# One-bank PSUM tiles, 512-token units and two more weights decoded early, in a fused attention, expert and gated-MLP kernel

## The chip, the cores and the metric

The kernel runs on one core of one Trainium2 chip. The metric is the device time of one execution in microseconds (us). Before the change it is 957.31 us, the median of three runs (956.15 to 957.85).

## The reference

Four batches of 576 tokens with 8 heads of 64 go through kernelized attention, then an expert layer, then a gated MLP; all in float32.

```python
def phi(x):
    proj = np.einsum('bhsd,df->bhsf', x, w_phi)                  # 64 -> 128
    proj = proj - np.max(np.abs(proj), axis=-1, keepdims=True)
    return np.concatenate([np.exp(proj), np.exp(-proj)], axis=-1)
kv = np.einsum('bhsf,bhsd->bhfd', k_p, v); z = np.sum(k_p, axis=2)
attn = num / den                                                # 2304 x 512 in all
e_idx = argmax(x @ w_gate)                                      # 8 experts, 512 -> 1024 -> 512
out[mask] = gate_w * eom * (np.maximum(x[mask] @ w1[e], 0) @ w2[e])
xn = x / rms * rms_g
out = (silu(xn @ w_gate) * (xn @ w_val)) @ w_out                # 512 -> 1536 -> 512
```

## The kernel before

There are two stages. **Stage 1** does attention, the gate and the expert layer for the four batches (0 to 3). Expert products start while the attention of the next batch still runs. The kernel guesses one expert per batch and computes all its tokens with it; a branch behind the stage (`general`, L899) would do the rest and is not entered by these inputs. **Stage 2** is the gated MLP. It goes over the 2304 tokens in units of `UT` = 384, six in all, in the order 0, 5, 1, 2, 3, 4 (L1031).

Nothing here is ordered by the compiler: each stage puts tasks with an engine, a modelled duration, a priority and the buffers they read and write into a `Graph` (L42). `emit` (L121) takes the task that can start first, and the instructions of each engine then stand in that order. A task also needs a free slot of each buffer tag it writes. The engines run their queues in order; semaphores follow from the tiles an instruction touches.

A float32 product is made of three float32r products (high by high, high by low, low by high). So weights and activations are kept as pairs, made by a cast on ACT and a subtraction on DVE. The MLP weights come as 64-bit floats: `decode` (L770) loads 128x1024 words into a `raw` buffer (two of them) and turns them into a pair, by one ACT instruction (L777), three of DVE (L779, L782, L785), a cast on ACT (L788) and a subtraction on DVE (L789). One step f of the MLP needs two decodes for gate and value (`decode_gv`, L792) and one for the output weights (`decode_o`, L799). Six of the twelve steps (`NPRE`) have their gate and value weights decoded in stage 1; all other decodes run during the first unit of stage 2.

`unit` (L846) does, for each of 12 steps, gate and value products (2 x 12 matmuls of 128x384, L860), silu on ACT (L866), the product with the value on DVE (L868), a cast (L870) and a subtraction (L871), then for each 128 tokens three output matmuls of 128x512 (L878). `prep` (L802) normalizes the tokens of the next unit into `xn` pairs, with one matmul for the mean square (L832).

PSUM has eight banks of 512 float32 per partition. `psum` (L299) makes four tiles of one bank (`ps0` to `ps3`) and two tiles of two banks each (`pq0`, `pq1`). The two-bank tiles take the projections of the attention (tag `pp`), which DVE reads whole (L414, L416). After nine projections `pq1` is taken out of `pp` and its two halves go to `ph`, the tag of the expert products (`mm1` L675, `mm2` L685), which then has three banks: `ps3` and the two halves of `pq1`. In stage 2 the gate and value products use `ps3` and three halves of `pq1` and `pq0`:

```python
self.ps = one + [t[:, i] for t in self.two[::-1] for i in range(2)]     # L303
self.g.retire("pp", 9, self.two[1], "ph", [self.two[1][:, i] for i in range(2)])   # L310
g.slot("po", kk.ps[0:3]); g.slot("pgv", kk.ps[3:7]); g.slot("pms", kk.ps[7:8])     # L1020 to L1022
```

In an expert product of 128x288 (12 matmuls, L682, or 24, L691) ACT and DVE read the bank afterwards: ACT L729 and DVE L731 make the pair `h`, DVE L743 makes `y`. Each step of the expert weights is itself a cast on ACT of 128x1024 (L712) and a subtraction on DVE (L713).

All transfers are issued from SP's queue. At the start these are the two halves of `w_phi` (L296), then keys, values and the left-over 64 tokens of each head (L367, L373, L382, L388).

Of the kernel before, what the change touches and what calls it, by code (L numbers as in the profile page):

```python
# [22 lines left out]
DM = H * D  # L23
P = 128
# [17 lines left out]
class Graph:  # L42
# [22 lines left out]
    def free_slot(self, b):  # L65
        self.slots[b.tag].append((b.end, b.slot[1], b.slot[2]))
        rule = self.leaving.get(b.tag)
        if rule:
            rule[0] -= 1
            for f in [f for f in self.slots[b.tag] if f[2] is rule[1] and rule[0] <= 0]:  # L70
                self.slots[b.tag].remove(f)
                n = 100 + len(self.slots[rule[2]])
                self.slots[rule[2]].extend((f[0], n + i, a) for i, a in enumerate(rule[3]))
                del self.leaving[b.tag]
# [153 lines left out]
class K:  # L228
# [62 lines left out]
    def attn_consts(self, c):  # L291
# [3 lines left out]
        for i in range(2):  # L295
            self.g.t("SP", 0.6, lambda i=i: nc.sync.dma_start(self.wraw[i * D:(i + 1) * D], self.w_phi),  # L296
                     w=[self.cBw], prio=0.5, nbytes=1 << 15)

    def psum(self, ctx):  # L299
        ps = self.pool(ctx, "ps", space=PSUM)  # L300
        self.two = [ps.tile([P, 2, 512], F32, name=f"pq{i}") for i in range(2)]
        one = [ps.tile([P, 512], F32, name=f"ps{i}") for i in range(4)]
        self.ps = one + [t[:, i] for t in self.two[::-1] for i in range(2)]  # L303
        self.g.slot("pa", one[0:3])
        self.g.slot("pp", self.two)
        self.g.slot("ph", one[3:4])

    def halve(self):

        self.g.retire("pp", 9, self.two[1], "ph", [self.two[1][:, i] for i in range(2)])  # L310
# [8 lines left out]
    def moe_slots(self, ctx):  # L319
        p = self.pool(ctx, "moe", side="right")  # L320
        self.moe_consts(p)
        self.mk(p, "xh", 2, [P, 2, NC, S], F32R)
# [35 lines left out]
    def attn(self, b, prio):  # L358
# [3 lines left out]
        xp = [Buf(None, 0) for _ in range(NC + 1)]  # L362

        def load(src, pr, np_):
# [6 lines left out]
            for i, m in enumerate((self.k, self.q)):  # L371
                for j in range(2):
                    g.t("SP", 0.6, lambda i=i, j=j, m=m: nc.sync.dma_start(  # L373
                        t.ap[j * 64:(j + 1) * 64, i], m[b, j::2, MAIN:S].rearrange("h t d -> t h d")),
                        w=[t], prio=np_, nbytes=LEFT * H * D * 2)
# [73 lines left out]
        el = vl = None  # L449
        for i, pr in enumerate([0, "L", 1, 2, 3]):  # L450
# [18 lines left out]
            if el is None:  # L469
                continue  # L470
            for pr, e, v, np_ in ready:
                pk, ks, pz = g.buf("pa"), g.buf("ks"), g.buf("pa")
                for j in range(2):
                    def kvm(j=j, pr=pr, e=e, v=v, pk=pk):
                        ops = [(v.ap[:, j, c], e.ap[:, at(j, c)]) for c in range(NC)]
                        ops.append((vl.ap[:, j, pr], el.ap[:, (pr % 2) * 2 + pr // 2]))
                        return [partial(nc.tensor.matmul, pk.ap[0:D + 1, j * 256:(j + 1) * 256], lhsT=v_,
                                        rhs=e_.rearrange("p f e -> p (f e)"), start=(n == 0), stop=(n == NC))
                                for n, (v_, e_) in enumerate(ops)]
                    g.t("PE", 5 * 0.431, kvm, r=[e, v, el, vl], rw=[pk], prio=np_, kind="pass", steps=5)  # L480
# [271 lines left out]
    def phase2_slots(self, ctx):  # L752
# [3 lines left out]
        self.xn = [p.tile([P, 2, UT], F32R, name=f"xn{i}") for i in range(NXN)]  # L756
        self.sq = p.tile([P, 2, UT], F32, name="sq")
        self.rm = p.tile([P, 2, UT], F32, name="rm")
        self.raw = [p.tile([P, 1024], U32, name=f"raw{i}") for i in range(2)]
        self.tt = [p.tile([P, 512], F32, name=f"tt{i}") for i in range(2)]  # L760
        self.ww = [p.tile([P, 512], F32, name=f"ww{i}") for i in range(3)]
# [3 lines left out]
    def use_phase2(self, g):  # L765
        for tag, aps in (("yu", [self.y]), ("sq", [self.sq]), ("rm", [self.rm]), ("raw", self.raw), ("tt", self.tt),
                         ("ww", self.ww)):
            g.slot(tag, aps)

    def decode(self, g, src, dst, dstap, prio):  # L770

        nc = self.nc
        raw, tt, ww = g.buf("raw"), g.buf("tt"), g.buf("ww")
# [14 lines left out]
        g.t("ACT", act(512, False), lambda: nc.scalar.copy(dstap(0), ww.ap), r=[ww], w=[dst], prio=prio)  # L788
        g.t("DVE", dve(512), lambda: nc.vector.tensor_tensor(out=dstap(1), in0=ww.ap, in1=dstap(0), op=ALU.subtract),  # L789
            r=[ww], rw=[dst], prio=prio)  # L790

    def decode_gv(self, g, f, prio):  # L792
        for i, m in enumerate((self.mg, self.mv)):
            src = (lambda ap: ap.rearrange("p (c n) -> p c n", c=NC),
                   m[:, f * 256:(f + 1) * 256].rearrange("(c p) n -> p c n", p=P))
            self.decode(g, src, self.wgv[f], lambda a, i=i, f=f: self.wgv[f].ap[:, i, a].rearrange("p c n -> p (c n)"),
                        prio)
# [4 lines left out]
    def prep(self, g, u, prio, hold=False):  # L802

        nc = self.nc
        y, sq, ms, rm = g.buf("yu"), g.buf("sq"), g.buf("pms"), g.buf("rm")
        g.t("SP", 0.5, lambda: nc.sync.dma_start(y.ap, self.ydr[:, :, u * UT:(u + 1) * UT]),
            r=self.yB, w=[y], prio=prio, nbytes=P * NC * UT * 4)
        self.prep_rest(g, y, sq, ms, rm, prio)
        xn = []
        for c in range(NC):  # L810
            x = g.buf("xn", hold)
            xn.append(x)
            g.t("DVE", dve(UT), lambda c=c: nc.vector.scalar_tensor_tensor(  # L813
                out=y.ap[:, c], in0=y.ap[:, c], scalar=self.gcol[:, c:c + 1], in1=rm.ap[:, 0],
                op0=ALU.mult, op1=ALU.mult), r=[rm], rw=[y], prio=prio)
        for c in range(NC):
            x = xn[c]
            g.t("ACT", act(UT, False), lambda x=x, c=c: nc.scalar.copy(x.ap[:, 0], y.ap[:, c]), r=[y], w=[x], prio=prio)
            g.t("DVE", dve(UT), lambda x=x, c=c: nc.vector.tensor_tensor(  # L819
# [247 lines left out]
```

## Time and profile before

| | |
|---|---|
| median of three runs | 957.31 us (956.15 to 957.85) |
| the profiled execution: its own time, its span | 959.13 us, 957.5 us |
| mean granted clock of TensorE | 0.989 of full speed |
| busy: TensorE matmul, weight load | 914.5 us (96%), 835.9 us (87%) |
| busy: VectorE, ScalarE, GpSimd | 433.9 us (45%), 337.4 us (35%), 3.2 us |
| matmul instructions | 6044 |
| first gate product of stage 2 starts | 485.70 us |

The names are those of the profile: PE is TensorE's matmul, PEld its weight load, DVE VectorE, ACT ScalarE, POOL GpSimd, SP the queue that issues transfers. Busy time of PE is modelled and overlaps a little from one matmul to the next, so how fast matmuls follow each other is read from the starts of pieces in order of time, not from the mean length of one. An idle time stands with the work that ended last before it.

### The profile page before, as it was taken

Reading aid. Unit: us, or ns where it says so; the run is one execution under the profiler, and the core shown is the slowest. Engines: PE = TensorE matmul, PEld = TensorE weight load, DVE = VectorE, ACT = ScalarE, POOL = GpSimd, SP = SyncE. Lnnn points to the kernel's source line nnn. Section 1 sums busy time; section 2 is a strip of 40 time slices with the busy share of each in tenths; the row PEclk is TensorE's granted clock in tenths of the full one; section 3 lists DMA queues with packets and bytes.
Section 4 is the critical chain, followed back from the end, with each engine's and each line's share of the span. In section 5 each row is a group of like instructions: output and inputs, shape, how many; then the busy total and the mean of one; then the engine's idle time right before and its main releaser. Section 6 shows DMA issues by size and latency. Waiting matters only on the chain. (4 is left out here: it accounts for less than half of the span.)

```text
span 957.5 us, 14539 instructions
## 1 busy us (share of the span) xinstructions
PE 914.5 (96%) x6044; PEld 835.9 (87%) x6045; DVE 433.9 (45%) x826; ACT 337.4 (35%) x588; POOL 3.2 (0%) x23
## 2 busy tenths in 40 slices
PE   7988999999999998999989799999999999999998
PEld 5677799789889997898988789999999998999997
DVE  4454565556444547884248882322323133132111
ACT  4343435534433325543145551322223123122111
POOL 1000000000000000000000000000000000000000
PEclk9997999999999999999999989999999999999999
DMA  5313513421511146673145440002001002000000
GB/s 147 105 56 109 139 47 117 143 62 45 180 56 55 49 159 200 181 231 102 48 135 156 148 139 34 1 1 67 1 1 66 1 1 67 1 1 34 1 1 34
DMA packets 84984, 74.60 MB, mean 78 GB/s; under 512 B 30256, under 2 KB 78512, under 8 KB 84400
## 3 DMA queue, kind: packets, MB, share of 16 engines
q1 hardware_dynamic: 84912, 73.60, 25.2%
q8 instruction: 50, 0.82, 0.4%
q14 instruction: 22, 0.18, 0.1%
HBM read 54.63 MB, written 18.96 MB: 77 GB/s over the span
## 5 line engine op out<-in xcount | busy, mean ns | idle before, releaser
L860 PE MATMUL pq<-xn,wgv 128*128 128x384 f32 x1296 | 240.0, 338 | 12.3 <-DVE sil L868 12.3
L860 PEld LDWEIGHTS pq<-xn,wgv 128*128 128x128 f32 x1296 | 227.1, 189 | 18.5 <-DVE sil L868 9.2
L878 PE MATMUL ps<-wo,a 128*128 128x512 f32 x648 | 160.5, 392 | 0.0
L868 DVE TENSOR_TENSOR sil<-pq,sil 128x384 f32<-128x384 f32 x71 | 39.6, 557 | 223.9 <-PE pq L860 223.9
L878 PEld LDWEIGHTS ps<-wo,a 128*128 128x128 f32 x648 | 120.7, 188 | 22.0 <-DVE a L871 0.2
L860 PE MATMUL ps<-xn,wgv 128*128 128x384 f32 x432 | 81.2, 335 | 2.5 <-PEq L914 2.5
L860 PEld LDWEIGHTS ps<-xn,wgv 128*128 128x128 f32 x432 | 75.9, 188 | 5.3 <-issue 2.7
L682 PE MATMUL pq<-xh,w 128*128 128x288 f32 x492 | 73.3, 300 | 7.4 <-DVE h L731 7.1
L691 PE MATMUL pq<-h,w 128*128 128x288 f32 x528 | 76.5, 298 | 2.8 <-DVE y L743 2.2
L870 ACT CAST a<-sil 128x384 fp32r<-128x384 f32 x72 | 36.8, 512 | 118.7 <-DVE sil L868 118.7
L682 PEld LDWEIGHTS pq<-xh,w 128*128 128x128 f32 x492 | 66.4, 188 | 10.7 <-DVE h L731 7.5
L691 PEld LDWEIGHTS pq<-h,w 128*128 128x128 f32 x528 | 71.3, 188 | 4.4 <-DVE y L743 3.1
L209 PE MATMUL ps<-kv,qp 128*128 128x65 f32 x512 | 69.2, 276 | 5.7 <-DVE x L444 4.5
L209 PEld LDWEIGHTS ps<-kv,qp 128*128 128x128 f32 x512 | 67.6, 201 | 7.8 <-DVE x L444 4.9
L414 DVE TENSOR_REDUCE m<-pq 128x8 f32<-128x1024 f32 x36 | 43.9, 1223 | 49.6 <-PE pq L410 45.9
L209 PE MATMUL ps<-e,v 128*65 128x256 f32 x256 | 63.2, 389 | 0.7 <-ACT e L465 0.7
L871 DVE TENSOR_TENSOR a<-sil,a 128x384 fp32r<-128x384 f32 x72 | 39.9, 555 | 28.8 <-ACT a L870 28.4
L209 PEld LDWEIGHTS ps<-e,v 128*65 128x65 f32 x256 | 35.0, 142 | 19.3 <-issue 1.8
L712 ACT CAST w<-wr 128x1024 fp32r<-128x1024 f32 x32 | 33.5, 1047 | 45.6 <-PE pq L691 18.5
L713 DVE TENSOR_TENSOR w<-wr,w 128x1024 fp32r<-128x1024 f32 x32 | 39.2, 1224 | 20.5 <-ACT w L712 19.8
L866 ACT ACTIVATE sil<-ps 128x384 f32<-128x384 f32 x35 | 17.2, 491 | 85.6 <-PE ps L860 85.6
L433 ACT ACTIVATE qp<-ps 128x512 f32<-128x512 f32 x64 | 34.7, 598 | 33.6 <-PE ps L209 30.1
(141 smaller groups left out, 985.7 us busy)
## 6 DMA issues: line engine op xcount, KB each, us to landing
wr<-in_moe_w SPq DMA_DIRECT2D x32, 512.0 KB, 3.7
xdr<-xh SPq DMA_DIRECT2D x4, 2304.0 KB, 9.4
raw<-in_moe_w_gate SPq DMA_DIRECT2D x12, 512.0 KB, 3.5
raw<-in_moe_w_val SPq DMA_DIRECT2D x12, 512.0 KB, 4.2
raw<-in_moe_w_out SPq DMA_DIRECT2D x12, 512.0 KB, 3.7
yu<-ydr SPq DMA_DIRECT2D x6, 768.0 KB, 4.9
qk<-in_k SPq DMA_DIRECT2D x16, 256.0 KB, 3.5
v<-in_v SPq DMA_DIRECT2D x32, 128.0 KB, 2.6
```

Of the source, the lines that this page charges most:

```text
L209: f()
L414: g.t("DVE", dve(1024), lambda: nc.vector.tensor_reduce(out=m.ap, in_=pv(), axis=AX.X, op=ALU.max, apply_absolute_value=True), r=[pp], w=[ ...
L433: g.t("ACT", act(512), lambda f=f: nc.scalar.activation(qp.ap[:, f].rearrange("p c t -> p (c t)"), pd.ap, AF.Exp, scale=1.0 - 2.0 * f), r= ...
L682: self.nc.tensor.matmul(ph[:, 0:HS], lhsT=wv[:, a, c, fs], rhs=xh[:, x, c, cs], start=(c == 0 and i == 0), stop=(c == NC - 1 and i == 2))
L691: self.nc.tensor.matmul(ph[:, 0:HS], lhsT=wv[:, a, f], rhs=hs[f][:, x, cs], start=(f == 0 and i == 0), stop=(f == 7 and i == 2))
L712: g.t("ACT", act(1024, False), lambda: nc.scalar.copy(w.ap[:, 0], wr.ap), r=[wr], w=[w], prio=pr - AHEAD)
L713: g.t("DVE", dve(1024), lambda: nc.vector.tensor_tensor(out=w.ap[:, 1], in0=wr.ap, in1=w.ap[:, 0], op=ALU.subtract), r=[wr], rw=[w], prio= ...
L860: nc.tensor.matmul(ps.ap[:, 0:UT], lhsT=w[:, i, a, c], rhs=xn[c].ap[:, x], start=(c == 0 and n == 0), stop=(c == NC - 1 and n == 2))
L868: g.t("DVE", dve(UT), lambda sil=sil, ps=pgv[1]: nc.vector.tensor_tensor(out=sil.ap, in0=ps.ap[:, 0:UT], in1=sil.ap, op=ALU.mult), r=[pgv[ ...
L870: g.t("ACT", act(UT, False), lambda sil=sil, a=a: nc.scalar.copy(a.ap[:, 0], sil.ap), r=[sil], w=[a], prio=pr)
L871: g.t("DVE", dve(UT), lambda sil=sil, a=a: nc.vector.tensor_tensor(out=a.ap[:, 1], in0=sil.ap, in1=a.ap[:, 0], op=ALU.subtract), r=[sil], ...
L878: nc.tensor.matmul(po[t].ap, lhsT=a.ap[:, x, ts], rhs=w[:, y], start=(f == 0 and n == 0), stop=(f == NF - 1 and n == 2))
```

## The change

- PSUM is made of one-bank tiles wherever a half is used by itself. When `pq1` leaves `pp`, its pool is closed and a new pool with two one-bank tiles (`ph0`, `ph1`) takes its place; before stage 2 all pools are closed and eight one-bank tiles (`pz0` to `pz7`) are made, four for output (`po`), four for gate and value (`pgv`). The mean square of `prep` has no bank of its own any more and takes one of `pgv`.
- Stage 2 has units of 512 tokens: four of them, and one of 256 (the left-over tokens of all batches), in the order 0, 4, 1, 2, 3. There are four `xn` tiles instead of five.
- The gate and value weights of steps 6 and 7 are decoded in stage 1, into a buffer `xh` that held the tokens of a batch (`keep`, `part`). Four decodes leave the first unit of stage 2.
- Scratch tiles are shared: eight tiles `row` of 128x512 for what were `tt`, `ww`, `sil`, `osb` and `rm`; the squares of `prep` are kept in a `raw` buffer.
- The key-value products of the first pair of heads are split: the part of the main tokens is issued before the left-over tokens are there.
- In batch 0 the two loads of `w_phi` and the four loads of left-over keys and queries are issued from ACT's queue instead of SP's.

```diff
-    def psum(self, ctx):
+    def psum(self):
+        self.banks, self.pair = ExitStack(), ExitStack()
+        p = self.pool(self.banks, "ps", space=PSUM)
+        one = [p.tile([P, 512], F32, name=f"ps{i}") for i in range(4)]
+        two = [p.tile([P, 2, 512], F32, name="pq0"),
+               self.pool(self.pair, "pq", space=PSUM).tile([P, 2, 512], F32, name="pq1")]
...
     def halve(self):
-        self.g.retire("pp", 9, self.two[1], "ph", [self.two[1][:, i] for i in range(2)])
+        self.pair.close()
+        p = self.pool(self.pair, "ph", space=PSUM)
+        return [p.tile([P, 512], F32, name=f"ph{i}") for i in range(2)]
+    def psum2(self, ctx):
+        self.pair.close()
+        self.banks.close()
+        p = self.pool(ctx, "pz", space=PSUM)
+        return [p.tile([P, 512], F32, name=f"pz{i}") for i in range(8)]
...
-            self.g.t("SP", 0.6, lambda i=i: nc.sync.dma_start(self.wraw[i * D:(i + 1) * D], self.w_phi),
-                     w=[self.cBw], prio=0.5, nbytes=1 << 15)
+            self.g.t("ACT", 0.6, lambda i=i: nc.scalar.dma_start(self.wraw[i * D:(i + 1) * D], self.w_phi),
+                     w=[self.cBw], prio=-2, nbytes=1 << 15)
...
+        eng, dma = ("ACT", nc.scalar.dma_start) if b == 0 else ("SP", nc.sync.dma_start)
...
             if el is None:
+                first = g.buf("pa")
+                for j in range(2):
+                    kv_part(j, *ready[0], first, range(NC))
                 continue
...
+    def part(self, f):
+        n = 4 * NC * P
+        return self.kept.ap.rearrange("p a c s -> p (a c s)")[:, (f - NPRE) * n:(f - NPRE + 1) * n].rearrange(
+            "p (i a c n) -> p i a c n", i=2, a=2, c=NC)
...
     def prep(self, g, u, prio, hold=False):
-        y, sq, ms, rm = g.buf("yu"), g.buf("sq"), g.buf("pms"), g.buf("rm")
+        y, sq, ms, rm, ri = g.buf("yu"), g.buf("raw"), g.buf("pgv"), g.buf("row"), g.buf("row")
...
-UT = 384
-NU = B * S // UT
-NXN = 5
+UT = 512
+NROW = 8
+NU = 5
 NPRE = 6
+NKEEP = 2
+def width(u):
+    return UT if u < B else B * LEFT
...
+        kk.kept = g.buf("xh", hold=True)
+        for f in range(NPRE, NPRE + NKEEP):
+            kk.decode_gv(g, f, 2000 + f, [kk.kept])
...
-    g.slot("po", kk.ps[0:3])
-    g.slot("pgv", kk.ps[3:7])
-    g.slot("pms", kk.ps[7:8])
+    g.slot("po", banks[0:4])
+    g.slot("pgv", banks[4:8])
```

The order moves on every engine, since the planner makes it anew. Three places count here.

On PE, at the first expert product of batch 2 (line L682, now L706), the names are the PSUM tiles that are written. Before:

```order
L682 MATMUL ps3_84<-xh_0_99,w_0_111 128x288 x12
L682 MATMUL pq1_80<-xh_0_99,w_0_111 128x288 x24
L682 MATMUL ps3_84<-xh_0_99,w_0_111 128x288 x12
L682 MATMUL pq1_80<-xh_0_99,w_1_112 128x288 x24
L682 MATMUL ps3_84<-xh_0_99,w_1_112 128x288 x12
```

Now:

```order
L706 MATMUL ph1_520<-xh_0_91,w_0_117 128x288 x12
L706 MATMUL ps3_82<-xh_0_91,w_0_117 128x288 x12
L706 MATMUL ph0_519<-xh_0_91,w_1_118 128x288 x12
L706 MATMUL ph1_520<-xh_0_91,w_1_118 128x288 x12
L706 MATMUL ps3_82<-xh_0_91,w_1_118 128x288 x12
```

Two products in a row into one tile `pq1` have become two products into two tiles, `ph0` and `ph1`.

On DVE, at the first expert product of batch 3 (the subtractions of `h`, L731, now L755). Before:

```order
L731 SCALAR_TENSOR_TENSOR h_1_102<-ps3_84,h_1_102 128x288
L713 TENSOR_TENSOR w_0_111<-wr_0_109,w_0_111 128x1024
L731 SCALAR_TENSOR_TENSOR h_1_102<-pq1_80,h_1_102 128x288
L731 SCALAR_TENSOR_TENSOR h_2_103<-pq1_80,h_2_103 128x288
L731 SCALAR_TENSOR_TENSOR h_2_103<-ps3_84,h_2_103 128x288
```

Now:

```order
L755 SCALAR_TENSOR_TENSOR h_1_108<-ph1_520,h_1_108 128x288
L805 SCALAR_TENSOR_TENSOR row1_2982<-row0_2981,row1_2982 128x512
L802 SCALAR_TENSOR_TENSOR row6_2987<-raw1_2980,row6_2987 128x512
L737 TENSOR_TENSOR w_0_117<-wr_0_115,w_0_117 128x1024
L755 SCALAR_TENSOR_TENSOR h_1_108<-ps3_82,h_1_108 128x288
L755 SCALAR_TENSOR_TENSOR h_2_109<-ph0_519,h_2_109 128x288
L809 TENSOR_TENSOR xh_0_91<-row1_2982,xh_0_91 128x512
```

The four moved decodes (L799, L802, L805 and L809, the last into `xh`) now stand between the subtractions of this batch.

On SP, at the start of stage 2, the loads of the packed weights (L776, now L796). Before, the two buffers take turns:

```order
L776 DMA raw0_2970<-in_moe2_w_out 128x1024
L776 DMA raw1_2971<-in_moe2_w_gate 128x4x256
L776 DMA raw0_2970<-in_moe2_w_val 128x4x256
L776 DMA raw1_2971<-in_moe2_w_out 128x1024
L776 DMA raw0_2970<-in_moe2_w_gate 128x4x256
```

Now:

```order
L796 DMA raw0_2979<-in_moe2_w_out 128x1024
L796 DMA raw1_2980<-in_moe2_w_out 128x1024
L833 DMA yu_2974<-ydr_73 128x4x256
L796 DMA raw0_2979<-in_moe2_w_out 128x1024 x3
L796 DMA raw0_2979<-in_moe2_w_gate 128x4x256
L796 DMA raw0_2979<-in_moe2_w_val 128x4x256
L796 DMA raw0_2979<-in_moe2_w_out 128x1024
L796 DMA raw0_2979<-in_moe2_w_gate 128x4x256
L796 DMA raw0_2979<-in_moe2_w_val 128x4x256
L796 DMA raw0_2979<-in_moe2_w_out 128x1024
L796 DMA raw0_2979<-in_moe2_w_gate 128x4x256
L796 DMA raw1_2980<-in_moe2_w_val 128x4x256
```

Ten loads in a row go through `raw0` alone, because `prep` holds `raw1` for its squares until its mean product has run.

## Rows read from the trace of the kernel before

**Rows 1.** The page: span and instructions.

```profile
span 957.5 us, 14539 instructions
```

**Rows 2.** Busy time by stretch: stretch, length, engines (instructions), PEclk, DMA share, GB/s.

```profile
0.00:98.00 98.00, 84.14 (x652) 68.27 (x654) 44.45 (x77) 41.28 (x66) 3.21 (x23) 0.93 0.39 112
98.00:364.00 266.00, 265.92 (x2220) 238.77 (x2220) 141.71 (x320) 110.65 (x195) 0.00 (x0) 1.00 0.32 98
364.00:485.70 121.70, 109.23 (x787) 104.92 (x788) 73.97 (x130) 45.10 (x78) 0.00 (x0) 1.00 0.46 140
485.70:562.00 76.30, 67.36 (x347) 62.32 (x348) 62.55 (x113) 42.18 (x71) 0.00 (x0) 0.96 0.52 158
562.00:953.20 391.20, 387.87 (x2041) 361.63 (x2039) 110.79 (x187) 97.83 (x178) 0.00 (x0) 1.00 0.06 20
```

**Rows 3.** Groups by form on PE, 485.7 to 957.5: busy us, mean ns, idle before.

```profile
L860 PE MATMUL pq<-xn,wgv 128*128 128x384 f32 x1296 | 240.0, 338 | 12.3 <-DVE sil L868 12.3
L878 PE MATMUL ps<-wo,a 128*128 128x512 f32 x648 | 160.5, 392 | 0.0
L860 PE MATMUL ps<-xn,wgv 128*128 128x384 f32 x432 | 81.2, 335 | 2.5 <-PEq L914 2.5
```

**Rows 4.** Waits of PE, 364 to 485.7: us in total, times, longest.

```profile
PE pq L682 <- DVE h L731: 7.1, 9, 1.8
PE pq L691 <- DVE y L743: 2.2, 4, 0.6
PE pq L691 <- DVE flagf L647: 0.6, 1, 0.6
```

**Rows 5.** A later unit of stage 2: timeline (three rows), chain of waits (two rows).

```profile
651.09 3.29 PE L860 MATMUL pq<-xn,wgv 128*128 128x384 f32 x18
...
655.03 3.39 PE L860 MATMUL pq<-xn,wgv 128*128 128x384 f32 x18 [0.65 <-DVE sil L868]
...
658.26 2.21 PE L878 MATMUL ps<-wo,a 128*128 128x512 f32 x9
...
692.21 4.16 PE pq L860 x24
696.37 2.05 PE ps L878 x9
```

**Rows 6.** The long stop in the first unit: timeline, and busy time by stretch.

```profile
552.59 3.78 PE L860 MATMUL pq<-xn,wgv 128*128 128x384 f32 x12 [6.19 <-DVE sil L868]
...
550.00:555.00 5.00, 2.41 (x8) 2.44 (x9) 4.49 (x10) 2.42 (x5) 0.00 (x0) 0.50 0.67 206
```

**Rows 7.** Expert products without attention beside them: timeline, PE and DVE.

```profile
374.52 0.46 DVE L731 SCALAR_TENSOR_TENSOR h<-pq,h 128x288 fp32r<-128x288 f32 x1 [1.65 <-ACT h L729]
...
376.02 3.42 PE L682 MATMUL pq<-xh,w 128*128 128x288 f32 x24 [1.75 <-DVE h L731]
...
469.56 3.32 PE L691 MATMUL ps<-h,w 128*128 128x288 f32 x24
...
472.71 4.94 PE L691 MATMUL pq<-h,w 128*128 128x288 f32 x36
...
478.21 1.84 PE L691 MATMUL pq<-h,w 128*128 128x288 f32 x12 [0.55 <-DVE y L743]
```

**Rows 8.** Groups by form on DVE, 364 to 562: the four instructions of a decode.

```profile
L782 DVE SCALAR_TENSOR_TENSOR ww<-raw,ww 128x512 uint32<-128x512 uint32 x35 | 24.1, 687 | 0.2
L785 DVE SCALAR_TENSOR_TENSOR ww<-tt,ww 128x512 uint32<-128x512 uint32 x34 | 23.3, 685 | 0.0
L789 DVE TENSOR_TENSOR wgv<-ww,wgv 128x512 fp32r<-128x512 f32 x24 | 16.5, 686 | 1.4 <-ACT wgv L788 1.4
L779 DVE TENSOR_SCALAR ww<-raw 128x512 uint32<-128x512 uint32 x35 | 14.7, 422 | 2.9 <-DMA raw<-in_moe_w_val 1.9 <-DMA raw<-in_moe_w_out 0.8
```

**Rows 9.** Waits of PE, 0 to 100: us in total, times, longest.

```profile
PE ps L400 <- DMA qk<-in_k: 3.3, 3, 1.9
```

**Rows 10.** The tile `raw`, 485 to 562: loads from issue to landing.

```profile
DMA to landing us min/median/max: 3.4/3.6/5.1
```

More of the change, by code (lines that the diff above doesn't have):

```diff
@@ L449, in attn, with kv_part, fn @@
         el = vl = None
+        def kv_part(j, pr, e, v, np_, pk, part):
+            def fn():
+                ops = [(v.ap[:, j, c], e.ap[:, at(j, c)]) if c < NC else
+                       (vl.ap[:, j, pr], el.ap[:, (pr % 2) * 2 + pr // 2]) for c in part]
+                return [partial(nc.tensor.matmul, pk.ap[0:D + 1, j * 256:(j + 1) * 256], lhsT=v_,
+                                rhs=e_.rearrange("p f e -> p (f e)"), start=(c == 0 and (pr > 0 or j == 0)), stop=(c == NC), skip_group_check=True)
+                        for c, (v_, e_) in zip(part, ops)]
+            g.t("PE", len(part) * 0.431, fn, r=([e, v] if 0 in part else []) + ([el, vl] if NC in part else []),
+                rw=[pk], prio=np_, kind="pass", steps=len(part))
         for i, pr in enumerate([0, "L", 1, 2, 3]):
@@ L469, in attn @@
             if el is None:
+                first = g.buf("pa")
+                for j in range(2):
+                    kv_part(j, *ready[0], first, range(NC))
                 continue
             for pr, e, v, np_ in ready:
-                pk, ks, pz = g.buf("pa"), g.buf("ks"), g.buf("pa")
+                pk, ks, pz = first if pr == 0 else g.buf("pa"), g.buf("ks"), g.buf("pa")
                 for j in range(2):
[L474 to L480, printed above, removed]
+                    kv_part(j, pr, e, v, np_, pk, (NC,) if pr == 0 else range(NC + 1))
                 g.t("ACT", act(512), lambda pk=pk, ks=ks: nc.scalar.copy(ks.ap, pk.ap[0:D + 1]),
@@ L812, in prep @@
             xn.append(x)
[L813 to L819, printed above, removed]
-                out=x.ap[:, 1], in0=y.ap[:, c], in1=x.ap[:, 0], op=ALU.subtract), r=[y], rw=[x], prio=prio)
+            g.t("ACT", act(n, False), lambda x=x, c=c: nc.scalar.copy(x.ap[:, 0, 0:n], y.ap[:, c, 0:n]),
+                r=[y], w=[x], prio=prio)
@@ new lines, in prep_rest @@
+        row = lambda t: lambda: t.ap[:, 0:n]
+        add(lambda: sv()[:, 0], lambda: sv()[:, 1], rw=[sq])
+        add(row(rm), row(ri), r=[ri], rw=[rm])
+        add(lambda: sv()[:, 0], row(rm), r=[rm], rw=[sq])
+        g.t("PE", n * 4 / 2400.0, lambda: nc.tensor.matmul(ms.ap[:, 0:n], lhsT=self.mean, rhs=sv()[:, 0],
+                                                           start=True, stop=True), r=[sq], w=[ms], prio=prio)
+        g.t("ACT", 1.3 + act(n), lambda: nc.scalar.activation(ri.ap[:, 0:n], ms.ap[:, 0:n], AF.Sqrt, bias=self.eps),
+            r=[ms], rw=[ri], prio=prio)
@@ L1010, in build @@
     moe.close()
+    banks = kk.psum2(ctx)
     p = kk.pool(ctx, "p2", side="right")
```

122 lines of the change are left out of this document (61 added, 61 removed).

## The prediction

> **What bounds the kernel now.** I read the stretches first. Between 98 and 364 us TensorE's matmul row is busy for 265.92 of 266 us, and from 562 us to the end of its work for 387.87 of 391.2 [rows 2]. So the kernel is a queue of matmuls with few holes, and a change pays only by making the matmuls shorter or by closing holes. The holes are in three places: the first 98 us (13.9 us idle), the stretch from 364 to 485.7, where attention is over and only expert products are left (12.5 us), and the first unit of stage 2 (8.9 us) [rows 2]. Then I asked what ended the waits. In the expert stretch they are waits for DVE, and every row names the tile pq, none ps, though a third of the products goes to ps3 [rows 4]. In stage 2 the same: 12.3 us before products into pq, all of it for DVE [rows 3]. A product into one half of a two-bank tile waits until DVE has read the other half. A tile counts as one thing, though the two halves are two banks.
>
> How fast matmuls follow each other comes from starts. In a full stretch 24 of 384 columns take 4.16 us, 173.3 ns each, and 9 of 512 columns take 2.05 us, 227.8 ns each [rows 5]. A stop costs more than its idle time: 36 products of 384 start at 651.09 and the next kind starts at 658.26, 7.17 us where 36 x 173.3 ns are 6.24. So 0.93 us are lost where the row says 0.65 [rows 5]. I add 0.28 per stop in stage 2 and, not having measured it there, 0.25 in the expert stretch.
>
> **Stage 2, the matmuls.** Output products keep their number (648) and width. Gate and value products are 1728 of 384 columns now: 299.5 us. After the change they are 4 x 288 = 1152 of 512 columns, 262.4 us at 227.8 ns, and 288 of 256 columns. That width in float32r is not in the trace. The line through 384 and 512 gives 118.8 ns; half of a 512 one, 113.9, is the low end and the spacing of 288 columns, 24 in 3.15 us or 131.3 ns [rows 7], the high end. I take 118.8, since the two points it comes from are the same instruction: 34.2 us. Sum 296.6, **2.9 us less** (between 4.3 less and 0.7 more). The Trainium skill, page "TensorE: Matmul & The Clock Gate", section "Back-to-back issue gap", gives columns over 2.4 plus 2.5 ns; by it 384 columns take 162.5 ns and the change would save only 0.7 us here, so that the sum below would be 932.9. The trace disagrees at 384 columns (173.3), and the measurement decides.
>
> **Stage 2, the stops.** One wait is 6.19 us [rows 6]; the nine others share 12.3 - 6.2 = 6.1 us. With one-bank tiles no product has to wait for the reader of another bank. With its own bank a product waits for a reader two steps back, which has long ended. Nine stops: 6.1 + 9 x 0.28 = **8.6 us less**. The long one has a second cause: DVE is busy for 62.55 of the 76.3 us around it [rows 2], because a decode costs it 0.42 + 3 x 0.69 = 2.48 us [rows 8], and the product's reader stands in its queue behind decodes. After the wait TensorE ran at 0.50 of its clock [rows 6]: the 12 products took 3.78 us instead of 2.08. In all 6.19 + 1.70 = **7.9 us less**, if DVE gets room: the first unit grows to 12 x (24 + 12) x 227.8 ns = 98.4 us, and DVE has 20 decodes (49.6 us), 24 operations of 512 columns for the steps (16.6 at 0.69) and some 10 us of preparation in it, 76 of 98. What is late next: the boundaries of units. There are four xn tiles now instead of five, so all of the next unit's pairs are made while the last output products run (5.5 us in a 512 unit, 2.7 in the 256 unit), four casts and four subtractions of about 0.6 to 0.7 each; and ACT's squares wait for a load of 1 MB ahead of the next silu. I charge 0.5 us for each of four boundaries, **2 us more** (0 to 8). Stage 2 together: 17.4 less.
>
> **Stage 1, the expert stretch.** Four of the waits for the reader y and one for flagf are pure waits across halves, 2.8 us and 5 x 0.25: 4.0 us go. Of the nine for h (7.1 us) part is real: at 376.02 PE had been idle 1.75 us, since 374.27, while the bank's own reader ended at 374.98 [rows 7], so some 0.7 us of 1.75 would have stayed. I take half of the 7.1 and of 9 x 0.25: 4.7. The four moved decodes put 9.9 us on DVE in batch 3's first product, some 16 x 1.6 = 26 us long, among its 16 subtractions. The order shows them between the readers; with three banks a reader may be two products late, so I charge only 1 us. Together **7.7 us less** (13.4 if all goes, 1 if the decodes take the place of the halves). Their loads (4 x 512 KB) fall where transfers use 0.46 of the engines and cost nothing; without that cover each is one load, 3.6 us [rows 10].
>
> **The first 98 us.** Six of SP's loads move to ACT, so the third and fourth key loads go out some five issues earlier; PE waits 3.3 us for keys [rows 9]. Against it stands that the order of the whole front is new, that ACT starts its first table load behind six issues, and that this stretch has lost 7% of its clock [rows 2], which can go either way. I take half of the 3.3, **1.5 us less** (7 less to 6 more), the splitting of the first pair with it. Moved priorities, the shared scratch tiles and the retired means cost nothing as long as a row tile is free; if one is not, it shows as a wait of ACT for an output transfer.
>
> **Sum.** -17.4 - 7.7 - 1.5 = -26.6. The rows are from an execution of 959.13 us, 1.6 above its span of 957.5 [rows 1] and 1.8 above the median of 957.31. Off the median: **930.7 us**.
>
> **The rivals.**
> *The one raw buffer (slower).* In the first unit ten loads in a row go through raw0. The weights of output step 7 are the eleventh after the first and are needed when 10 gate-value steps (5.47 us each) and 7 output steps (2.73) are done, 73.8 us into the stage. With a cycle of c per load they are ready at 12c + 1.4, so c may be 6.0. It is a load of 3.6 us (up to 5.1 [rows 10]) plus the two DVE instructions that read the buffer (1.1) plus what stands before them: about 5.3. Above 6.0 each us of c costs 12 us on PE. At 7 it gives 943; from 8.3 it takes back all of the 26.6 and the kernel is slower. For it: the waits of DVE's queue in a full unit. Against: that unit now has 22 us of free DVE. 8% for a part, 5% for slower.
> *The tail does not give.* DVE was what PE waited for, and it gets four more decodes there: a gain of 1 instead of 7.7, 937.4. 12%.
> *The front grows.* A later start of the first expert product or a longer stretch at half clock, 6 instead of -1.5: 938.2. 12%.
> *The halves still count as one.* Then 8.6 of stage 2 and 7.7 of stage 1 stay: 947. The order shows separate names, so 3%. The Trainium skill, page "PSUM — Partial Sum Buffer", section "PSUM bank collisions raise a hardware error", says that engines may not meet in one bank but may in different banks, so the chip itself asks for no wait between halves; no run here shows that yet.
>
> **How the numbers follow.** The forecast has 60%, by itself 922 to 939. The range goes up to 945 to take in the tail, the front and the partial raw case and down to 920 for more real gain in the expert stretch; left out are the halves, the slow raw case and the outermost ends, under 2 in 10. About 0.2% (1.9 us) is what a measurement here can tell. Faster by more: all but the slow raw case and a chance sum near zero, 0.93; same 0.02; slower 0.05.
>
> **What would show it.** Right: no wait of PE for DVE before products into ph or pz in the expert stretch and at unit starts; gate products of 512 columns 228 ns apart and of 256 about 119; no half clock in the first unit; stage 2 some 450 us from first to last matmul instead of 467.5. Wrong: a hole of PE for DVE or ACT in the second half of the first unit with ACT waiting for raw (the raw buffer); waits before ph with DVE at decodes of xh (the tail); more idle time or a lower clock before 98 us (the front).

## The result and the profile after

The changed kernel takes 927.39 us, the median of four runs (924.22 to 931.33), against 957.57 beside it (956.15 to 957.85): a ratio of 0.969, 95% interval 0.965 to 0.9729, or 30.2 us less. The forecast was 930.7, with 920 to 945 as its range. The profiled execution took 928.17 us, 30.96 less than the one before.

The page and the busy time by stretch, cut where the same work stands as in [rows 2]: front, attention with expert products, expert products alone, and stage 2 by units (first, second, the other three).

```profile
span 926.6 us, 13852 instructions
```

```profile
0.00:98.00 98.00, 90.44 (x662) 75.97 (x664) 46.49 (x96) 40.87 (x68) 3.21 (x23) 0.90 0.42 121
98.00:364.00 266.00, 266.00 (x2238) 239.23 (x2237) 144.73 (x313) 113.14 (x195) 0.00 (x0) 1.00 0.32 99
364.00:472.60 108.60, 103.11 (x762) 101.03 (x762) 79.13 (x135) 49.13 (x86) 0.00 (x0) 1.00 0.51 156
472.60:571.00 98.40, 98.39 (x430) 80.78 (x431) 67.51 (x117) 45.81 (x76) 0.00 (x0) 1.00 0.38 117
571.00:624.00 53.00, 53.00 (x369) 49.17 (x369) 20.85 (x37) 17.34 (x35) 0.00 (x0) 1.00 0.09 34
624.00:922.30 298.30, 298.30 (x1300) 243.55 (x1298) 75.37 (x103) 63.47 (x99) 0.00 (x0) 1.00 0.05 17
```

Stage 2 starts at 472.61 us instead of 485.70, 13.1 earlier, and takes 449.7 us from its first to its last matmul instead of 467.5, 17.8 less. In it PE's row is full: 98.39 of 98.40 us in the first unit, where [rows 2] had 67.36 of 76.30. All of PE's waits from 364 us on, which answer to [rows 4] and to the waits of [rows 3]:

```profile
PE pz L894 <- PEq L948: 2.2, 1, 2.2
PE ps L706 <- DVE h L755: 2.0, 3, 1.0
PE ph L706 <- DVE h L755: 1.4, 2, 0.7
```

The first is the passage from stage 1 to stage 2, which was 2.5 before. The other two are 3.4 us in the expert stretch where 10 were: not the "no wait before ph" that the forecast named as its sign. Stage 2 has no wait of its own left. How fast matmuls follow each other, in the chain of waits (start, us, line, number), against [rows 5]:

```profile
583.52 2.86 PE pz L894 x24
...
605.57 2.83 PE pz L894 x24
...
645.70 5.48 PE pz L894 x24
...
911.32 5.51 PE pz L894 x24
916.83 5.50 PE pz L912 x24
```

The first two lie in the unit of 256 tokens: 119.2 and 117.9 ns a product. Those of 512 columns stand 228.3 to 229.6 ns apart.

One thing did not get better, the clock of the front: 0.90 in the first 98 us, where [rows 2] had 0.93. The mean granted clock of the four runs went from 0.983 to 0.994, and the slowest run is the one with the lowest. Span times clock is 914 to 917 us in all four, so below I give the clock beside the time.

### The profile page after: what moved, and what is told of

The parts are those of the page before. It is cut to its first block, busy times and chain, and to the rows that moved or that the text cites. A ratio compares the mean times of both kernels' runs of the same rounds, so it can differ in the third digit from the quotient of the medians.

```text
span 926.6 us, 13852 instructions
## 1 busy us (share of the span) xinstructions
PE 909.3 (98%) x5754; PEld 789.7 (85%) x5755; DVE 434.5 (47%) x798; ACT 330.1 (36%) x558; POOL 3.2 (0%) x23
## 5 line engine op out<-in xcount | busy, mean ns | idle before, releaser
L894 PE MATMUL pz<-xn,wgv 128*128 128x512 f32 (+1 forms) x1200 | 256.2, 369 | 2.2 <-PEq L948 2.2
L894 PEld LDWEIGHTS pz<-xn,wgv 128*128 128x128 f32 x1200 | 209.9, 188 | 42.4 <-issue 2.4
L912 PE MATMUL pz<-wo,a 128*128 128x512 f32 x648 | 159.4, 394 | 0.0
L912 PEld LDWEIGHTS pz<-wo,a 128*128 128x128 f32 x648 | 121.0, 188 | 27.3 <-issue 1.4
L715 PE MATMUL ph<-h,w 128*128 128x288 f32 x576 | 82.4, 297 | 0.0
L715 PEld LDWEIGHTS ph<-h,w 128*128 128x128 f32 x576 | 77.5, 188 | 0.5
L706 PE MATMUL ph<-xh,w 128*128 128x288 f32 x480 | 70.5, 299 | 1.4 <-DVE h L755 1.4
L706 PEld LDWEIGHTS ph<-xh,w 128*128 128x128 f32 x480 | 65.0, 188 | 3.0 <-DVE h L755 1.8
L894 PE MATMUL pz<-xn,xh 128*128 128x512 f32 (+1 forms) x240 | 51.4, 369 | 0.0
L706 PE MATMUL ps<-xh,w 128*128 128x288 f32 x288 | 43.5, 300 | 2.0 <-DVE h L755 2.0
```

Source lines behind the costliest of these rows:

```text
L706: self.nc.tensor.matmul(ph[:, 0:HS], lhsT=wv[:, a, c, fs], rhs=xh[:, x, c, cs], start=(c == 0 and i == 0), stop=(c == NC - 1 and i == 2))
L715: self.nc.tensor.matmul(ph[:, 0:HS], lhsT=wv[:, a, f], rhs=hs[f][:, x, cs], start=(f == 0 and i == 0), stop=(f == 7 and i == 2))
L894: nc.tensor.matmul(ps.ap[:, 0:UT], lhsT=w[:, i, a, c], rhs=xn[c].ap[:, x, 0:UT], start=(c == 0 and n == 0), stop=(c == NC - 1 and n == 2))
L912: nc.tensor.matmul(po[t].ap, lhsT=a.ap[:, x, ts], rhs=w[:, y], start=(f == 0 and n == 0), stop=(f == NF - 1 and n == 2))
```

## The experiments

Times are medians; clock is the lowest and highest mean granted clock of a kernel's runs; stage 2 is first to last matmul; the idle times of PE are summed from the timeline of the profiled run, for the first 100 us and for the stretch from 364 us to stage 2, without the passage to stage 2 itself.

| kernel | us (lowest to highest) | clock | stage 2 | idle, first 100 us | idle, expert stretch |
|---|---|---|---|---|---|
| before (the nine runs beside h, i and j) | 957.46 (956.20 to 960.98) | 0.984 to 0.989 | 467.5 | 13.8 | 10.0 |
| changed | 927.39 (924.22 to 931.33) | 0.983 to 0.994 | 449.7 | 7.5 | 3.3 |
| a_onebank | 934.88 (932.23 to 936.46) | 0.983 to 0.991 | 459.9 | 10.6 | 0.4 |
| b1_halves_expert | 939.95 (938.13 to 942.76) | 0.985 to 0.992 | 451.3 | 8.2 | 9.6 |
| b2_halves_stage2 | 940.66 (938.58 to 943.92) | 0.984 to 0.991 | 464.7 | 9.0 | 2.8 |
| c_nokeep | 923.00 (921.85 to 927.59) | 0.986 to 0.994 | 452.4 | 7.9 | 1.7 |
| d_384 | 935.89 (933.22 to 937.91) | 0.983 to 0.989 | 459.6 | 7.7 | 1.2 |
| e_front_sp | 921.64 (919.07 to 924.64) | 0.989 to 0.997 | 449.7 | 7.4 | 2.8 |
| f_nosplit | 928.32 (927.52 to 929.60) | 0.985 to 0.990 | 451.3 | 9.5 | 3.4 |
| g_oneraw | 932.96 (931.56 to 936.30) | 0.981 to 0.985 | 452.6 | 7.7 | 2.9 |
| h_after | 927.68 (925.16 to 930.12) | 0.984 to 0.992 | 451.3 | 8.7 | 3.1 |
| h_front_sp | 921.09 (919.94 to 922.09) | 0.995 to 0.999 | 449.9 | 7.1 | 3.4 |
| i_front_sp_nokeep | 921.09 (916.36 to 922.62) | 0.990 to 0.999 | 450.5 | 8.3 | 1.0 |
| j_fill | 920.35 (917.45 to 922.40) | 0.997 to 1.000 | 450.9 | 8.0 | 1.7 |

### One-bank tiles alone, in the kernel before

```diff
-        self.g.retire("pp", 9, self.two[1], "ph", [self.two[1][:, i] for i in range(2)])
+        self.pair.close()
+        p = self.pool(self.pair, "ph", space=PSUM)
+        return [p.tile([P, 512], F32, name=f"ph{i}") for i in range(2)]
...
-    g.slot("po", kk.ps[0:3])
-    g.slot("pgv", kk.ps[3:7])
-    g.slot("pms", kk.ps[7:8])
+    g.slot("po", banks[0:3])
+    g.slot("pgv", banks[3:7])
+    g.slot("pms", banks[7:8])
```

> The kernel before with one edit: PSUM in one-bank tiles for the expert products (two tiles where there were halves of pq1) and in stage 2 (eight tiles). Every engine keeps its order, units stay at 384, no decode is moved. Theory (a half of a two-bank tile waits for the reader of the other half): the nine short stops of stage 2 go, 8.6 us; in the expert stretch 8.7 us of idle time go (the forecast's 7.7 and the 1 us that it charged for moved decodes); the long stop of 6.2 us and its half clock stay, since DVE is as full as before. Together 17 us less, about 940. Rival 1 (the gain came from the new order and the shared tiles are harmless): 957, within 2 us. Rival 2 (the long stop was the halves too): 25 us less, about 932.

Measured 934.88, a ratio of 0.9758 (0.9733 to 0.9782): 22.5 us less, more than the 17 of the theory. PE's waits from 364 us on, and the timeline of PE at the wait that is left:

```profile
PE pz L874 <- DVE sil L882: 7.0, 1, 7.0
PE pz L874 <- PEq L928: 2.3, 1, 2.3
PE ph L696 <- DVE h L745: 0.4, 1, 0.4
```

```profile
534.54 3.90 PE L874 MATMUL pz<-xn,wgv 128*128 128x384 f32 x12 [7.04 <-DVE sil L882]
```

The nine short stops of stage 2 are gone, and the long one stays with its 12 products at half speed (3.90 us for what takes 2.08): stage 2 is 7.5 us shorter, though the long stop grew from 6.2 to 7.0. So rival 2 falls. What the theory had too small is the expert stretch: of 10 us of idle time 0.4 are left. From the first product of batch 2 (367.61 us before, 365.34 in a) to stage 2 it is 118.1 us before and 105.3 in a, 12.8 less. The products write the banks in the same order in both kernels, `ph0` where the first half of `pq1` was, so this is not a better choice of bank. The readers are earlier. A pair of products into the two halves, and ACT's read of the first half, before and then in a:

```profile
369.29 3.35 PE L682 MATMUL pq<-xh,w 128*128 128x288 f32 x24
372.68 0.41 ACT L729 ACTIVATE h<-pq 128x288 fp32r<-128x288 f32 x1 [1.98 <-PE pq L682]
```

```profile
367.02 3.34 PE L696 MATMUL ph<-xh,w 128*128 128x288 f32 x24
368.82 0.41 ACT L743 ACTIVATE h<-ph 128x288 fp32r<-128x288 f32 x1 [0.40 <-PE ph L696]
```

Before, ACT reads the first half 3.39 us after the pair has started, when the product into the second half has ended too; in a it reads `ph0` after 1.80 us, when that product alone has ended. So a shared tile holds up both sides: a product waits for the reader of the other half, and a reader waits for the product into the other half. DVE's timeline shows what the long stop waits for:

```profile
533.25 0.68 DVE L799 SCALAR_TENSOR_TENSOR ww<-tt,ww 128x512 uint32<-128x512 uint32 x1
533.85 0.55 DVE L882 TENSOR_TENSOR sil<-pz,sil 128x384 f32<-128x384 f32 x1
```

From 523 to 534 us DVE works through decodes and the next unit's preparation, with no more than 0.9 us of idle time at a stretch, and the reader of the bank (L882) stands behind them.

### The halves back, one place at a time

In the changed kernel, `halve` returns the halves of `pq1` again (b1); or two of the four gate and value banks of stage 2 are halves of one tile (b2). Every engine keeps the order of the changed kernel.

```diff
...
-        self.pair.close()
-        p = self.pool(self.pair, "ph", space=PSUM)
-        return [p.tile([P, 512], F32, name=f"ph{i}") for i in range(2)]
+        return [self.pq1[:, i] for i in range(2)]
```

```diff
-        return [p.tile([P, 512], F32, name=f"pz{i}") for i in range(8)]
+        t = p.tile([P, 2, 512], F32, name="pt")
+        z = [p.tile([P, 512], F32, name=f"pz{i}") for i in range(6)]
+        return z[0:5] + [t[:, 0], t[:, 1]] + z[5:6]
```

> The changed kernel with one edit undone: the expert products use the two halves of pq1 again. Order, stage 2 and moved decodes as in the changed kernel. Theory: PE's idle time between the end of attention and stage 2 goes up by about 8 us (5 to 13), with waits for DVE at h and y; stage 2 still takes 449.7 us; total about 935. Rival (the stretch is short because of the new order): no more than 1 us of more idle time there, total 927.

> The changed kernel with one edit undone: in stage 2 two of the four gate and value banks are halves of one two-bank tile, the other six banks are tiles by themselves. Same order. In it 13 products into one half follow straight on a product into the other half. Theory: each stops for the reader on ACT or DVE, some 0.8 us of idle time and 0.28 lost around it, 14 us in all (10 to 18); stage 2 takes 460 to 468 us instead of 449.7; total about 941. Rival (the stops went because DVE had room): stage 2 stays at 450, total 927.

b1 measured 939.95, b2 940.66, 12.6 and 13.3 more than the changed kernel. PE's largest waits from 364 us on, of b1 and then of b2:

```profile
PE pq L704 <- DVE h L753: 5.5, 6, 2.3
PE pz L892 <- PEq L946: 2.6, 1, 2.6
PE pq L713 <- DVE y L765: 2.2, 4, 0.6
PE pq L713 <- DVE h L753: 1.0, 2, 0.7
...
```

```profile
PE pt L896 <- ACT row L902: 7.1, 11, 0.7
PE pz L896 <- PEq L950: 1.9, 1, 1.9
PE pt L896 <- DVE row L904: 1.7, 2, 0.9
...
PE pt L896 <- ACT row L869: 0.8, 1, 0.8
```

In b1 the waits for h and y are back under the name pq, and stage 2 starts 8.3 us later than in the changed kernel's profile, as the theory had it. The whole is more than its 935: in the profiled runs (938.13 against 928.17) the other 1.6 us are a lower clock at the start of stage 2, and the medians lie another 2.6 us apart. In b2 every wait inside stage 2 bears the name pt, and the stage is 15.0 us longer: 9.6 of idle time in 14 stops, 14 x 0.28 = 3.9 around them, and a stretch of lower clock at its start (1.7). Both rivals fall. The tile is the unit of waiting, not the bank.

### The moved decodes and the width of a unit

c decodes steps 6 and 7 in the first unit again (and `xh` is an ordinary pair of buffers), d has six units of 384.

```diff
...
-NKEEP = 2
+NKEEP = 0
...
```

```diff
...
-UT = 512
+UT = 384
...
-NU = 5
+NU = 6
...
-    return UT if u < B else B * LEFT
+    return UT
```

> The changed kernel with no step moved: the gate and value weights of steps 6 and 7 are decoded in the first unit again, 24 decodes there instead of 20; units of 512 and one-bank tiles stay. DVE then has 24 x 2.48 = 59.5 us of decodes, 16.6 of steps and some 10 of preparation in the first unit, 86 of 98 us. Theory (the longer unit gives the room): no long stop, stage 2 at most 2 us longer; stage 1 up to 1 us shorter; total 926 to 929. Rival (the moved decodes closed the long stop): a stop of several us in the second half of the first unit and half clock behind it, stage 2 some 8 us longer, total about 935.

> The changed kernel with units of 384 in stage 2 (six of them); one-bank tiles, moved decodes, shared tiles and the front stay. Theory (forecast's terms): the gate and value products cost 2.9 us more (1728 at 173.3 ns instead of 1152 at 228.3 and 288 at 118.6), one boundary more costs nothing; the first unit is 74.5 us long with 20 decodes (49.6 us of DVE), 12.5 of steps and 8 of preparation, 70 of 74.5, so some wait for DVE comes back there: 0 to 5 us. Stage 2 takes 452 to 458 us, total 930 to 936. Rival 1 (moving four decodes is enough to close the long stop at this width): only the 2.9, stage 2 452.6, total 930. Rival 2 (only the longer unit closes it): a stop of 5 to 7 us for DVE and half clock after it, stage 2 461, total 938.

c measured 923.00, d 935.89. PE's waits for DVE and ACT in stage 2 are, in c and then (with the longest stop's line of PE's timeline) in d:

```profile
PE pz L911 <- DVE wo L808: 0.6, 2, 0.3
```

```profile
PE pz L894 <- DVE row L902: 3.8, 2, 2.8
...
PE pz L912 <- ACT wo L808: 1.2, 1, 1.2
...
PE pz L894 <- DVE xn L846: 0.5, 1, 0.5
PE pz L912 <- DVE wo L809: 0.2, 1, 0.2
```

```profile
534.69 3.79 PE L894 MATMUL pz<-xn,wgv 128*128 128x384 f32 x12 [2.77 <-DVE row L902]
```

With 512 columns and all 24 decodes there is no long stop, only 0.6 us; with 384 columns and 20 decodes 5.7 us of idle time come back in five stops, one with half clock behind it, and stage 2 is 9.9 us longer. So the longer unit by itself closes the long stop; the moved decodes by themselves do not, though the longest stop is 2.8 us in d where it was 7.0 in a. c's stage 2 is 2.7 us longer, 1.2 of it by the two stops and the rest by a lower clock at its start, which the changed kernel has in one profile (h_after in the table, 451.3) and not in the other (449.7). Its expert stretch has 1.7 us less idle time. The early decodes gain nothing: without them the span times the clock is 914.3 (median) against 915.2.

a and d measure almost the same (934.88 and 935.89). So at 384 columns the moved decodes and all else that is new add nothing in sum to the one-bank tiles, which gave 22.5 us, and the step from d to the changed kernel, 8.5 us by the medians, is what the longer unit gave.

### The raw buffer

In stage 2 all 20 decodes go through raw0, and raw1 holds the squares alone.

```diff
...
+    g.slots["sq"], g.slots["raw"] = g.slots["raw"][1:], g.slots["raw"][:1]
```

> The changed kernel with a harder case of the raw-buffer rival: in stage 2 all 20 decodes go through raw0 alone, raw1 keeps the squares. In the changed kernel the loads that went through raw0 alone were issued 4.93 us apart. Theory (the forecast's formula, used for the last load): 20 x 4.93 us and a decode behind it end about 4.3 us after the 95.7 us at which the last output weights are needed; a stop of 2 to 8 us at the end of the first unit, stage 2 452 to 458 us, total 930 to 935. Rival (the order puts other products ahead and hides it, or the buffer is no limit): stage 2 stays within 1 us of 449.7, total 927.

In the changed kernel the ten loads through raw0 alone are issued from 479.70 to 524.65 us, 5.0 us apart on average (SP's timeline, the first row holds three of them):

```profile
479.70 11.10 SPq L796 DMA_DIRECT2D raw<-in_moe_w_out  x3
495.06 0.38 SPq L796 DMA_DIRECT2D raw<-in_moe_w_gate  x1
...
514.51 0.37 SPq L796 DMA_DIRECT2D raw<-in_moe_w_val  x1
519.89 0.34 SPq L796 DMA_DIRECT2D raw<-in_moe_w_out  x1
524.65 0.37 SPq L796 DMA_DIRECT2D raw<-in_moe_w_gate  x1
```

That is under the 6.0 from which the rival would have cost time, and nothing waits. In g PE stops at the end of the first unit:

```profile
563.80 0.50 PE L912 MATMUL pz<-wo,a 128*128 128x512 f32 x1 [1.59 <-ACT wo L808]
564.52 2.79 PE L912 MATMUL pz<-wo,a 128*128 128x512 f32 x11 [0.22 <-DVE wo L809]
```

Stage 2 is 452.6 us, 2.9 longer and within the theory's bounds. The whole is 5.6 us longer by the medians; the rest goes with the lower clock of these runs (0.981 to 0.985). The rival's mechanism is there; in the change it has about 1 us per load to spare.

### The front

e and h_front_sp issue the six first loads from SP again; f leaves the products of the first pair in one piece; i takes away both ACT's loads and the early decodes; j adds 16 matmuls on a constant, whose results nothing reads, to i. h_after is the changed kernel, on the same chip as h_front_sp, i and j.

```diff
-            self.g.t("ACT", 0.6, lambda i=i: nc.scalar.dma_start(self.wraw[i * D:(i + 1) * D], self.w_phi),
-                     w=[self.cBw], prio=-2, nbytes=1 << 15)
+            self.g.t("SP", 0.6, lambda i=i: nc.sync.dma_start(self.wraw[i * D:(i + 1) * D], self.w_phi),
+                     w=[self.cBw], prio=0.5, nbytes=1 << 15)
...
-        eng, dma = ("ACT", nc.scalar.dma_start) if b == 0 else ("SP", nc.sync.dma_start)
+        eng, dma = ("SP", nc.sync.dma_start)
...
```

```diff
...
-                first = g.buf("pa")
-                for j in range(2):
-                    kv_part(j, *ready[0], first, range(NC))
                 continue
...
```

```diff
...
+        for i in range(n):
+            w = self.g.buf("ph")
+            k = self.g.t("PE", 0.24, lambda w=w: self.nc.tensor.matmul(
+                w.ap[:, 0:P], lhsT=self.mean, rhs=self.mean, start=True, stop=True), rw=[w], prio=60)
+            k.ready = t0 + (t1 - t0) * i / n
...
```

> The changed kernel with one edit undone: the two loads of w_phi and the four loads of left-over keys and queries of batch 0 are issued from SP again, with the old priorities. Theory: the third and fourth key loads go out later, PE's waits for keys in the first 30 us go up from 2.3 us by 1 to 3 us, and idle time in the first 100 us from 7.5 to 9 to 11 us; total 1 to 3 us more, 928 to 930. Rival (the front is shorter because of the split first pair): idle time there stays at 7.5 (within 1), total 927.

> The changed kernel with one edit undone: the key-value products of the first pair of heads are one piece again, issued when the left-over tokens are there. Theory (the forecast gave the split nothing of its own): idle time of PE in the first 100 us stays at 7.5 us (within 1), total 927. Rival (the split fills a hole while left-over tokens are on their way): 16 products of 256 columns move from 16.8 us to behind the left-over keys, 3 to 4 us more idle time before 25 us, total about 931.

> The changed kernel as it is, again, beside the three others of this set. Its first four runs were 924.2 to 931.3 at a mean granted clock of 0.994 to 0.983; the span times that clock was 914 to 917 in each. All theories: 925 to 929, span times clock 914 to 917.

> The changed kernel with the six first loads on SP again, a second time. Its first run was 921.6, with the same idle time in the first 100 us as the changed kernel (7.35 against 7.52) but one stretch of half clock there instead of two. Theory 1 (loads on ACT cost time: they make two 1.0 us stops for ACT's qp, and a half-clock stretch of 10 us follows each): again 4 to 7 us less than the changed kernel in this set, with a mean clock higher by 0.004 or more. Rival (the half clock falls by chance, the loads are free): within 2 us of it and the same clock.

> The changed kernel with two parts undone: first loads on SP, and no step decoded early (24 decodes in the first unit). Theory: both effects add. Without the four decodes the expert stretch has 1.1 to 1.6 us less idle time, the first unit gets two stops of 0.3 us for wo; span times clock 0.5 to 1.5 below that with SP loads alone, total 919 to 921.5. Rival (the second 3.5 us lower median of the kernel without early decodes was clock by chance): within 1 us of the one with SP loads alone, or above it.

> As the kernel before in this set (SP loads, no early decodes), and 16 matmuls of 128x128 on a constant, which nothing reads, put on PE between 44 and 76 us of the plan where it has nothing to start; they write the free banks of the expert products. They take 16 x 0.23 = 3.7 us at full clock, part of it in the 2 to 3 us of idle time there. Theory 1 (half clock follows the stops of 0.5 to 1 us): no stretch at 0.50 between 44 and 90 us, mean clock 0.996 or more, total 2 to 5 us less. Rival (half clock comes with the short 65-column products whatever the stops): clock there as before, total 0 to 3 us more.

e came out against both of its theories: 921.64, 5.8 us below the changed kernel, with the same idle time. h repeats it on one chip: 921.09 against 927.68, all five runs of the one below all five of the other, the clock 0.995 to 0.999 against 0.984 to 0.992, and span times clock the same (medians 915.5 and 915.0). So the loads on ACT cost 6.6 us, and they cost it in clock. f measured 928.32, not to be told from the changed kernel; its idle time before 25 us is 5.8 us against 4.5 and 5.5 in the two profiles of the changed kernel, where the rival asked for 3 to 4 more, so the split is worth little.

Two stops in the timeline of PE between 50 and 70 us, in h_after and then in h_front_sp:

```profile
53.52 0.40 PE L584 MATMUL ps<-wgt,xh 128*64 128x8 f32 x4 [1.00 <-ACT qp L449]
53.94 3.62 PE L209 MATMUL ps<-kv,qp 128*128 128x65 f32 x16
```

```profile
51.44 0.66 PE L209 MATMUL ps<-ident,d 128*128 128x128 f32 x4 [0.54 <-DVE xl L460]
55.36 0.66 PE L209 MATMUL ps<-ident,x 128*128 128x128 f32 x4 [0.66 <-DVE xh L544]
```

In h_after 16 products of 65 columns take 3.62 us behind a stop of 1.00, where they take 2.00 at full clock. Busy time by stretch from 44 to 90 us, of the changed kernel, h_after, h_front_sp, i and j (the clock is the third number from the end):

```profile
44.00:90.00 46.00, 42.99 (x304) 39.38 (x305) 23.82 (x53) 19.21 (x34) 0.00 (x0) 0.78 0.35 116
```

```profile
44.00:90.00 46.00, 42.77 (x355) 38.27 (x354) 26.21 (x57) 19.76 (x35) 0.00 (x0) 0.89 0.42 136
```

```profile
44.00:90.00 46.00, 44.31 (x372) 39.38 (x371) 27.55 (x75) 20.95 (x39) 0.00 (x0) 0.93 0.39 133
```

```profile
44.00:90.00 46.00, 43.46 (x388) 37.99 (x387) 29.40 (x77) 21.14 (x39) 0.00 (x0) 1.00 0.40 134
```

```profile
44.00:90.00 46.00, 43.90 (x395) 38.69 (x395) 27.76 (x71) 19.79 (x37) 0.00 (x0) 1.00 0.39 133
```

b1 and b2, which have the loads on ACT and the stops for ACT's qp, show 0.93 there, as h_front_sp does. So which stops bring the fall is argued, not shown; that the kernel with the loads on ACT gets less clock is shown by five runs against five.

j's clock is 0.997 or more in all five runs, as its first theory had it. But its total, 920.35, is no better than i's 921.09: span times clock rose from 913.1 to 916.0, most of the 3.7 us of the added matmuls, and took back what the clock gave. i against h_front_sp is a tie (921.09 both), as its rival had it: 2.4 us less work by span times clock, and a lower clock in most runs. All three are faster than both kernels; j's ratio to the kernel before is 0.9598 (0.9576 to 0.9621).

## Why the prediction was right, step by step

The total was forecast as -26.6 us against -30.2 by the medians and -30.9 by the profiled runs. By its terms, in the profiled runs:

| term | forecast | measured |
|---|---|---|
| stage 2, matmuls | -2.9 | about -1.5 |
| stage 2, nine short stops | -8.6 | all gone |
| stage 2, long stop with its half clock | -7.9 | gone |
| stage 2, four boundaries | +2.0 | no idle time |
| stage 2 together | -17.4 | -17.8 |
| expert stretch | -7.7 | -9.1 (worked out below) |
| first 98 us, and all else in stage 1 | -1.5 | -4.0 (what is left) |

**Matmuls.** The 118.8 ns for 256 columns, a width that the trace of before did not show, was measured as 117.9 to 119.2. The wide ones were 228.3 to 229.6 instead of 227.8; with 229 and 118.6 the gate and value products take 298.0 us instead of 296.6. The Trainium skill, page "TensorE: Matmul & The Clock Gate", section "Back-to-back issue gap", gives columns over 2.4 plus 2.5 ns as the gap of an isolated matmul, an estimate of 109.2 ns at 256 columns. The prediction used it for a stream. The products here follow one another, each with a weight load of its own, and stand 117.9 to 119.2 ns apart, so the figure is too low for them at 256 columns as it was at 384.

**Stops.** Right, and shown from both sides: one-bank tiles alone remove them (a), halves alone bring them back (b1, b2). The rival that halves still count as one is out. The Trainium skill, page "Perfetto Trace Analysis", section "Matmuls", says that independent groups of matmuls should rotate through the banks, so that one is read while the next is filled; b2 is a case where they rotate and products wait all the same, since two of the banks share a tile.

**Long stop.** Right, and for the reason given, room for DVE in a longer first unit: c keeps the room without the moved decodes and has no long stop, d has the moved decodes without the room and keeps a stop of 2.8 us and the half clock behind it.

**Boundaries.** Charged 2 us, worth nothing: PE's row is full across all of them.

**Expert stretch.** The forecast let half of the h waits stay, with the argument that the bank's own reader was late too (374.98 us, where PE was ready at 374.27). That step was wrong. The own reader was late because the tile was shared: ACT's read of that half had waited until 372.68 for the product into the other half. In a, with the same banks in the same order, 0.4 us are left of 10, and the stretch is 12.8 us shorter, near the 13.4 that the forecast gave if all goes. Against that, the moved decodes cost more than the 1 us charged. From the first product of batch 2 to stage 2 the changed kernel needs 109.8 us and c 107.2: 2.7 us more, with three stops in batch 3 (1.65 us) that c does not have. The other two stops, 1.7 us in batch 2, stand in c as well and belong to the rest of the new order. The two errors nearly cancel: 8.2 us less than the 118.1 of before, and 9.1 if the mean product of stage 2, about 0.9 us, is set aside, which lies inside the stretch now and ahead of it before. 6.6 us less idle time and ten stops fewer at the forecast's 0.25 give the same 9.1.

**Front.** The sum came out better than forecast, 6.3 us less idle time less some 3 us of lower clock, but the step named for it was wrong. Moving the loads was to bring keys earlier and gain 1.5. PE waits 2.3 and 3.2 us for keys and queries with the loads on ACT (the changed kernel and h_after) and 3.1 and 2.9 with the loads on SP (e and h_front_sp), no clear gain; undoing the move leaves idle time as it was and gains 6.6 by the clock. Two places of the kernel before make up 5.2 of the 6.3 us: 1.7 us for keys and queries from 36.9 to 39.0 us, and a long stop for DVE, shown before and in the changed kernel:

```profile
74.37 4.04 PE L209 MATMUL ps<-kv,qp 128*128 128x65 f32 x18 [3.49 <-DVE x L444]
```

```profile
69.09 4.10 PE L209 MATMUL ps<-kv,qp 128*128 128x65 f32 x18 [0.34 <-DVE x L460]
```

a, with the old order, still has 2.26 and 2.02 us at these two places; e and f have no more than 0.33 at the long stop and wait for no load at the other. So neither the loads nor the split alone closed them. That the rest of the new order did is likely, not shown: both undone together was not run, and a and before, with the same order there, differ by 3 us themselves (10.6 and 13.8).

**Rivals.** The raw buffer was the right thing to price: 5.0 us per load, where the forecast put 5.3, against a limit of 6.0, and a stop at once when it is made tighter (g). The tail gave more than forecast, although its sign showed: stops before ps and ph with DVE at the moved decodes. The front did not grow in sum, though its clock fell as that rival had it.

## What to carry to other kernels

Where an engine waits for the reader of a buffer, look at the name of the tile before the name of the engine: if one half is written while the other is read, two tiles remove the wait with the order of the products untouched (22 of the 30 us here). And a reader that looks late in such a trace may be late only because it too waits for the other half, so its lateness is no reason to expect that the wait will stay. A change that alters the first microseconds should be judged by clock and idle time apart, since a few small stops that move can cost more clock than idle time. What a stage of decodes needs in order to be hidden is measured per unit: a longer unit gave DVE the room that moving decodes was meant to give.

## What the runs showed of the hardware that was not expected

- The clock that TensorE gets differs from run to run of one kernel: 0.983 to 0.994 for the mean of the changed kernel's first four runs, 924.2 to 931.3 us, with span times clock within 0.4%. In the profiled runs of this kernel the loss lies in the front (0.90 and 0.91 in the first 98 us) and, in h_after, at the start of stage 2 as well.
- Half clock (1.2 GHz, 0.50 in the rows) comes in the front behind stops as short as 1.00 us (h_after) or 0.66 (h_front_sp) among short products, but not behind each: i has the same two stops as h_front_sp (0.54 and 0.66) and a clock of 1.00. With constant matmuls in the gaps it did not come in the profiled stretch, and the mean of five runs was 0.997 to 1.000. The Trainium skill, page "TensorE: Matmul & The Clock Gate", section "A second HAM failure mode: psum-queue depth-cycling", tells of a kernel whose clock swings because of short idle times between groups of matmuls. h_after and h_front_sp agree with it; the full clock of i behind the same stops shows that the stops alone do not decide it.
